# The scores of A in two tiles of 64 rows side by side, half of the heads in each bank

## The chip, the cores and the metric

The kernel runs on one NeuronCore of a Trainium2 chip, as one launch. The metric is the device time of that launch in microseconds (us). The core's engines run side by side, each through its own stream of instructions in order: TensorE (PE in the profile, and PEld for its weight loads), VectorE (DVE), ScalarE (ACT), GpSimd (POOL) and SyncE (SP), which here only issues transfers. They wait for one another through semaphores. Matmul results land in PSUM, a memory of 8 banks over 128 partitions; DVE and ACT read them there.

## What is computed

Nyström attention over 8 batches of 8 heads, 576 tokens of width 64, and behind it a two-layer network with SiLU on all 4608 tokens (512 to 2048 to 512). Cut to what matters:

```python
q_lm = q.reshape(B, H, 32, 18, D).mean(axis=3)       # 32 landmarks per head
k_lm = k.reshape(B, H, 32, 18, D).mean(axis=3)
A  = softmax(scale * q    @ k_lm.T)                  # 576 x 32
Bm = softmax(scale * q_lm @ k_lm.T)                  # 32 x 32
C  = softmax(scale * q_lm @ k.T)                     # 32 x 576
Z = Bm.T / (norm1(Bm) * norminf(Bm) + 1e-6)
for _ in range(6):
    Z = 2 * Z - Z @ Bm @ Z
x = A @ Z @ C @ v                                    # then to (tokens, 512)
out = silu(x @ w_in) @ w_out
```

q, k and v are drawn with a standard deviation of 0.1. The softmax subtracts each row's maximum; any number that is the same for all terms of a row would do.

## The kernel before

**Stages.** The order of all instructions is written out by hand. Batch 0's attention runs alone at the start (lines 630 to 712). Then a loop over batches (717) takes 16 steps each; every step computes a piece of the hidden layer (`l1_mm`, tile `hps`), its SiLU on ACT (`l1_act`, tile `gT`) and some matmuls of the second layer (`l2_mm`, tile `ops`, copied out by ACT as `ost` and stored by SP). Between them stand the pieces of the next batch's attention. `d` is 4 for batch 0, 3 for batch 1 and 0 after; in step d + 1 the scores of B and C are computed, in step d + 2 those of A. `idle` issues matmuls of zeros that fill PE's time, `table` loads ACT's function table for Exp or Silu.

**Layout.** A batch's eight heads are two groups g of four. Each head has 32 landmarks and the 64 columns of D are split into two halves e of 32, so a group's four heads with one half lie on 4 x 32 = 128 partitions: `qkT` holds q and k that way, transposed (`transpose_qk`), and `bd` holds k's landmarks as a block diagonal of 128 x 128 for each g and e, with zeros outside the four 32 x 32 blocks (`bd_expand`).

**The scores of A** are computed in chunks of tokens, `TCH`: four whole chunks of 128 and one of 64. `a_scores(i)` makes scores for pair i: chunks 0 and 1 (i = 0), 2 and 3 (i = 1), and chunk 4 alone (i = 2). For every chunk, group and half it issues one matmul: weights `qkT` (128 rows, the chunk's 128 tokens), moving `bd` (128 rows, 128 columns), accumulated over e. That is 16 matmuls for the whole chunks and 4 for the last, where the weights have 64 columns. One PSUM bank, `sa[i]`, holds 2 chunks of 256 scores (8 heads of 32 landmarks): `sa[0]` in the pool `psa`, `sa[1]` in `pso`; the last chunk lies in the bank `bb` of the B work, or in `pso` for batch 0.

**What follows, pair by pair:** `a_max(i)` (L486, DVE) writes the negated maximum over 32 landmarks to `nm`; `a_shift(i)` (L493, PE) adds it to the bank with one matmul of the identity with `nm` broadcast; `a_exp(i)` (L499, ACT) writes the exponentials to `ex`. `a_norm(i)` is `a_sum` (L509, DVE, to `arec`), `a_rec` (L514, DVE) and `a_mul` (L524, POOL, to `an`). `an` is then transposed to `AT`, by PE and copies (`a_transpose`, `a_out`) for batches 0 and 1, by transfers of SP after that.

**Beside it on DVE and PE:** `c_scores` (PE, tile `scp`, tiles of 32*32), `c_max` (L382) and `c_exp` (L390) for C; `b_max`, `b_exp`, `b_norm`, `f_mm`, `b_scale` (L322) and `f_out` (L327) for B; then the iteration, alternately `ns_mm` (PE, `bb<-fx`) and `ns_step` (L348, DVE, `fx`); then `w_mm`, `w_out` (tiles `wp`, `W`), `x_out`, `z_mm`, `z_out`, and four `m_unit` (tiles `mp`, `mb`: 64*32 tiles on PE, copied by DVE and ACT), which give the weights of the hidden layer. `landmarks_pe` (`lmp`) sums rows of a later batch with the identity as weights; `landmarks_pool` does so on POOL from batch 3 on, behind a small copy (`gate`, L868) that waits for DVE.

Of the kernel before, what the change touches and what calls it, by code (L numbers as in the profile page):

```python
# [10 lines left out]
AF = mybir.ActivationFunctionType  # L11
# [28 lines left out]
def kernel(  # L40
# [9 lines left out]
    nc = tc.nc  # L50
    B, H, S, Dh = q.shape
    L = 32
    SEG = S // L
# [3 lines left out]
    sc = 1.0 / float(Dh) ** 0.5  # L57
# [3 lines left out]
    TCH = [(c, min(c + 128, S)) for c in range(0, S, 128)]  # L61
# [13 lines left out]
    def mm(o, lhsT, rhs, start, stop):  # L75
        nc.tensor.matmul(out=o, lhsT=lhsT, rhs=rhs, start=start, stop=stop,  # L76
                         skip_group_check=True)
# [4 lines left out]
    def psa1(nm, dt=FP):  # L82
        return psa.tile([128, 512 if dt == FP else 1024], dt, tag="a", name=nm)

    def pso1(nm, dt=FP):
        return pso.tile([128, 512 if dt == FP else 1024], dt, tag="o", name=nm)
# [98 lines left out]
    def landmarks_pe(b, p, j0, n, ts=(0, SEG)):  # L185

        o = p[:, 0:4 * Dh].rearrange("p (j d) -> p j d", d=Dh)[:, j0:j0 + n, :]
        for t in range(*ts):
            mm(o, ident, nat_t[b][:, j0:j0 + n, Dh * t:Dh * t + Dh],
               start=(t == 0), stop=(t == SEG - 1))  # L190
# [27 lines left out]
    class Att:  # L218
# [239 lines left out]
        def a_dims(self, i):  # L458
            cc = list(range(2 * i, min(2 * i + 2, len(TCH))))
            return cc[0], len(cc), TCH[cc[0]][1] - TCH[cc[0]][0]  # L460

        def a_scores(self, i):
            if i == 0:
                s = psa1("sa")
            elif self.b == 0:
                s = pso1("sa")
            else:
                s = pso1("sa") if i == 1 else self.bb[:, 128:384]
            self.sa[i] = s
            first = True  # L470
            for c in range(2 * i, min(2 * i + 2, len(TCH))):
                c0, c1 = TCH[c]
                o = 256 * (c - 2 * i)
                ov = s[0:c1 - c0, o:o + 256].rearrange("p (r g n) -> p g r n", r=2, g=2)
                for g in range(2):
                    for e in range(2):
                        mm(ov[:, g].rearrange("p r (j l) -> p r j l", l=L),
                           self.qkT[:, 2 * g, c0:c1, e],
                           self.bd[:, g, :, e].rearrange("p (j r l) -> p r j l", r=2, l=L),
                           start=first, stop=(e == 1))  # L480
                        first = False

        def a_max(self, i):
            c, n, pr = self.a_dims(i)
            with nc.allow_low_precision(reason="any shift common to a row's terms is exact"):
                nc.vector.tensor_reduce(  # L486
                    out=self.nm[0:pr, c:c + n, :],
                    in_=self.sa[i][0:pr, 0:256 * n].rearrange("p (c h l) -> p c h l", h=8, l=L),
                    op=OP.max, axis=AX.X, negate=True)

        def a_shift(self, i):
            c, n, pr = self.a_dims(i)
            mm(self.sa[i][0:pr, 0:256 * n].rearrange("p (c l) -> p c l", l=L), ident[0:pr, 0:pr],  # L493
               self.nm[0:pr, c:c + n, :].rearrange("p c h -> p (c h)").unsqueeze(2)
                   .to_broadcast((pr, 8 * n, L)), start=False, stop=True)

        def a_exp(self, i):
            c, n, pr = self.a_dims(i)
            nc.scalar.activation(out=self.ex[0:pr, c:c + n, :].rearrange("p c n -> p (c n)"),  # L499
                                 in_=self.sa[i][0:pr, 0:256 * n], func=AF.Exp, scale=sc / SEG)  # L500

        def a_part(self, i):
            c, n, pr = self.a_dims(i)
# [135 lines left out]
    a = Att(0)  # L639
# [13 lines left out]
    a.b_max()  # L653
    a.b_exp()
    a.a_start()
    a.a_scores(0)
    a.a_scores(1)
    a.a_scores(2)
    a.c_max(0)
    a.c_exp(0)  # L660
# [19 lines left out]
    a.a_exp(1)  # L680
    a.c_out(1, nc.scalar.copy)
    a.w_scale()
    a.a_norm(0)
    lp0 = ps2("lmp")
    idle(lp0[:, 1, :], 5)
    a.ns_step()
    a.ns_mm()
    landmarks_pe(1, lp0[:, 0, :], 1, 1, (0, 9))
    a.a_norm(1)
    a.ns_step()  # L690
    a.ns_mm()
# [25 lines left out]
    for b in range(B):  # L717
        nxt = b + 1 < B
        cnt = CNT.get(b, EVEN if b % 2 == 0 else ODD)
        h = {}  # L720
# [11 lines left out]
        for s in range(NDC):  # L732
# [39 lines left out]
            elif not nxt or s == d:  # L772
                l1(s)
                act(s)
                l2_mm(cnt[s])

            elif s == d + 1:
                l1(s)
                act(s)
                l2_mm(cnt[s])  # L780
                a.b_scores()
                a.c_scores()
                a.b_max()
                a.c_max(0)
                table(AF.Exp)
                a.b_exp()
            elif s == d + 2:
                n = cnt[s]
                a.a_start()
                a.a_scores(0)  # L790
                a.a_scores(1)
                a.c_max(1)
                a.a_max(0)
                a.a_max(1)
                a.c_exp(0)
                a.c_exp(1)
                l2_mm(min(n - 4, 6))
                a.a_scores(2)
                a.a_max(2)
                a.a_shift(0)  # L800
                a.a_exp(0)
                l2_mm(2)
                a.a_shift(1)
                a.a_exp(1)
                a.b_norm()
                l2_mm(2)
                a.a_shift(2)
                a.a_exp(2)
                l2_mm(n - 4 - min(n - 4, 6))
                table(AF.Silu)  # L810
                if b == 0:
                    a.f_mm()
                    a.b_scale()
                    a.f_out()
                l1(s)
            elif b == 0:
                l1(s)
                r = s - d
                if r == 3:
                    act(s - 1)  # L820
                    a.ns_mm()
                    a.c_transpose(0)
                    a.a_norm(0)
                    a.ns_step()
                    a.c_out(0)
                elif r == 4:
                    a.ns_mm()
                    a.c_transpose(1)
                    a.w_scale()
                    a.ns_step()  # L830
                    a.ns_mm()
# [132 lines left out]
```

## Time and profile before

| | us |
|---|---|
| median of 3 runs | 278.99 (278.54 to 279.84) |
| the profiled execution, its own time | 280.51 |
| its span in the trace | 278.8 |
| PE busy in the span | 264.3 (95%) |
| ACT, DVE, POOL busy | 176.9, 161.0, 117.4 |
| mean granted clock of PE | 0.967 |

The groups of the page that belong to the scores of A, all batches together:

```profile
L76 PE MATMUL sa<-bd,qkT 128*128 128x128 bf16 x128 | 8.8, 220 | 0.0
L486 DVE TENSOR_REDUCE nm<-sa 128x16 bf16<-128x512 f32 x16 | 10.3, 682 | 0.0
L76 PE MATMUL sa<-nm,ident 128*128 128x512 bf16 x16 | 6.4, 398 | 1.2 <-DVE nm L486 1.2
L499 ACT ACTIVATE ex<-sa 128x512 bf16<-128x512 f32 x16 | 9.4, 598 | 2.3 <-PE sa L76 2.0
L509 DVE TENSOR_REDUCE arec<-ex 128x16 f32<-128x512 bf16 x16 | 10.9, 679 | 0.4 <-ACT ex L499 0.3
```

A group's line gives the line of the kernel (L76 is the helper that issues every matmul), engine, operation, the tile written and those read, the shape of the PE tile as rows*columns, the shape of the data, how often; then the busy time in us and the mean of one in ns; then the idle time of the engine just before them and what ended it. Matmuls are pipelined: 220 ns is the time of one from start to end, and the next one starts long before. In a timeline a line gives start, duration, engine and operation; runs of one kind are merged with their number.

### The profile page before, as it was taken

Reading aid. Unit: us, or ns where it says so; the run is one execution under the profiler, and the core shown is the slowest. Engines: PE = TensorE matmul, PEld = TensorE weight load, DVE = VectorE, ACT = ScalarE, POOL = GpSimd, SP = SyncE. Lnnn points to the kernel's source line nnn. Section 1 sums busy time; section 2 is a strip of 40 time slices with the busy share of each in tenths; the row PEclk is TensorE's granted clock in tenths of the full one; section 3 lists DMA queues with packets and bytes.
Section 4 is the critical chain, followed back from the end, with each engine's and each line's share of the span. In section 5 each row is a group of like instructions: output and inputs, shape, how many; then the busy total and the mean of one; then the engine's idle time right before and its main releaser. Section 6 shows DMA issues by size and latency. Waiting matters only on the chain.

```text
span 278.8 us, 6934 instructions
## 1 busy us (share of the span) xinstructions
PE 264.3 (95%) x2826; PEld 149.1 (53%) x2826; DVE 161.0 (58%) x399; ACT 176.9 (63%) x350; POOL 117.4 (42%) x165
## 2 busy tenths in 40 slices
PE   5968999999999999998999999998999999999994
PEld 2845655565554555464645565454645565555541
DVE  4895688378586756839792757658784653100000
ACT  2354696578756975668666955687667855646511
POOL 8434232514796269365774279217741030100000
PEclk9775799999999999999999999999999999999998
DMA  6999998893992965649193948315291312110111
GB/s 105 204 208 206 204 207 172 141 177 58 177 179 61 172 131 94 124 92 192 56 156 71 196 115 114 92 42 93 27 179 38 91 54 72 40 75 38 40 75 75
DMA packets 37792, 32.37 MB, mean 116 GB/s; under 512 B 18816, under 2 KB 29056, under 8 KB 37760
## 3 DMA queue, kind: packets, MB, share of 16 engines
q0 software_dynamic: 15104, 18.35, 41.3%
q1 hardware_dynamic: 22656, 13.57, 19.9%
q8 instruction: 22, 0.36, 0.5%
q14 instruction: 10, 0.08, 0.1%
HBM read 36.70 MB, written 9.44 MB: 165 GB/s over the span
## 4 chain that ended last, share of the span: by engine, by line
PE 84%; DVE 9%; issue 2%; DMA 2%; ACT 1%; POOL 0%; ACTq 0%; POOLq 0%
PE ops L76 43%; PE hps L76 22%; PE bb L76 4%; PE mp L76 4%; PE lmp L76 3%; DVE cmx L382 3%; PE sa L76 3%; DMA nat<-in_q_dram 2%; PE scp L76 2%; PE wp L76 2%; DVE nm L486 1%; DVE fx L322 1%; PE atp L542 1%; PE idle L76 1%; PE ctp L404 1%
## 5 line engine op out<-in xcount | busy, mean ns | idle before, releaser
L76 PE MATMUL ops<-w_out_sb,gT 128*128 128x512 bf16 x576 | 148.9, 380 | 0.0
L593 ACT ACTIVATE gT<-hps 128x576 bf16<-128x576 f32 x128 | 82.4, 652 | 65.2 <-PE hps L76 64.9
L76 PE MATMUL hps<-AT,mb 128*128 128x288 bf16 x512 | 83.5, 288 | 0.4 <-DVE mb L565 0.2
L76 PEld LDWEIGHTS <-gT 128*128 128x128 bf16 x576 | 52.0, 98 | 48.0 <-issue 7.0
L76 PEld LDWEIGHTS <-mb 128*128 128x128 bf16 x512 | 48.4, 98 | 26.6 <-issue 2.0
L182 DVE STREAM_TRANSPOSE qkT<-nat 128x576 f32<-128x576 f32 x32 | 39.3, 1244 | 1.9 <-DMA nat<-in_k_dram 1.3
L524 POOL TENSOR_TENSOR an<-ex,arec 128x512 bf16<-128x512 bf16 (+1 forms) x24 | 21.2, 902 | 28.9 <-ACT W L433 14.8
L565 DVE CAST mb<-mp 128x512 bf16<-128x512 f32 x30 | 20.7, 691 | 20.1 <-PE mp L76 20.1
L619 ACT COPY ost<-ops 128x512 f32<-128x512 f32 x36 | 21.1, 586 | 10.7 <-PE ops L76 10.6
L348 DVE SCALAR_TENSOR_TENSOR fx<-fx,bb 128x320 bf16<-128x320 bf16 (+1 forms) x40 | 17.2, 430 | 17.8 <-PE bb L76 17.5
L204 POOL TENSOR_TENSOR lma<-nat 128x1152 f32<-128x1152 bf16 x10 | 23.7, 2373 | 0.0
L153 ACT ACT_TABLE_LOAD x16 | 20.5, 1283 | 1.1 <-PEq L948 0.8
L566 ACT CAST mb<-mp 128x512 bf16<-128x512 f32 x32 | 18.7, 584 | 3.8 <-PE mp L76 3.7
L245 POOL COPY bd<-lmc 32x128 bf16<-32x128 bf16 x28 | 8.1, 289 | 30.5 <-DVE lmc L237 29.7
L76 PE MATMUL bb<-fx 32*32 32x64 bf16 (+2 forms) x168 | 13.3, 211 | 4.3 <-DVE fx L327 3.1
L76 PEld LDWEIGHTS <-ident 128*128 128x128 bf16 (+1 forms) x240 | 12.5, 111 | 8.7 <-issue 5.3
L76 PEld LDWEIGHTS <-fx 32*32 32x32 bf16 (+1 forms) x168 | 8.3, 95 | 15.4 <-DVE fx L327 4.2
L868 POOL COPY gate<-nrm 128x2 f32<-128x2 f32 x6 | 1.1, 186 | 35.1 <-DVE nrm L318 31.8
L509 DVE TENSOR_REDUCE arec<-ex 128x16 f32<-128x512 bf16 (+1 forms) x24 | 14.1, 588 | 0.4 <-ACT ex L499 0.3
L76 PE MATMUL mp<-w_in_sb,zwT 64*32 64x512 bf16 x256 | 13.7, 400 | 0.1
L76 PE MATMUL lmp<-nat,ident 128*128 128x64 bf16 x216 | 10.9, 214 | 1.9 <-DMA nat<-in_k_dram 1.3
L382 DVE TENSOR_REDUCE cmx<-scp 128x1 f32<-128x576 f32 x16 | 12.0, 751 | 0.7 <-PE scp L76 0.4
(85 smaller groups left out, 264.2 us busy)
## 6 DMA issues: line engine op xcount, KB each, us to landing
out_dram<-ost SPq DMA_DIRECT2D x36, 256.0 KB, 2.3
nat<-in_k_dram POOLq DMA_DIRECT2D x16, 288.0 KB, 6.3
nat<-in_q_dram POOLq DMA_DIRECT2D x16, 288.0 KB, 7.6
v<-in_v_dram POOLq DMA_DIRECT2D x8, 576.0 KB, 7.6
w_in_sb<-in_moe_w_in_dram POOLq DMA_DIRECT2D x4, 512.0 KB, 15.6
w_out_sb<-in_moe_w_out_dram POOLq DMA_DIRECT2D x4, 512.0 KB, 16.2
AT<-an SPq DMA_TRANSPOSE x30, 4.4
eCT<-eC SPq DMA_TRANSPOSE x12, 5.7
```

The lines of the kernel that those rows point to most:

```text
L76: nc.tensor.matmul(out=o, lhsT=lhsT, rhs=rhs, start=start, stop=stop, skip_group_check=True)
L153: nc.scalar.activation(out=spare[:, 1:2], in_=spare[:, 0:1], func=func)
L182: nc.vector.transpose(out=o.rearrange("p (l t) -> p t l", t=SEG), in_=nat_t[b][:, j, :].bitcast(FP).rearrange("p (t l) -> p t l", l=L))
L204: nc.gpsimd.tensor_tensor(out=a1, in0=nat[:, :, 0:3 * w], in1=nat[:, :, 3 * w:6 * w], op=OP.add)
L348: nc.vector.scalar_tensor_tensor(out=n, in0=self.fx, scalar=2.0, in1=self.p, op0=OP.mult, op1=OP.subtract)
L382: nc.vector.tensor_reduce(out=mx, in_=self.s[g][:, :, 0:HF], op=OP.max, axis=AX.XY, negate=True)
L509: nc.vector.tensor_reduce(out=r, in_=x, op=OP.add, axis=AX.X)
L524: nc.gpsimd.tensor_tensor(out=self.an[0:pr, c:c + n, :].rearrange("p c (h l) -> p (c h) l", l=L), in0=x, in1=r.unsqueeze(2).to_broadcast(( ...
L565: (copy[0] if copy else nc.vector.tensor_copy)(out=o[:, 0, :], in_=m[0])
L566: nc.scalar.copy(out=o[:, 1, :], in_=m[1])
L593: nc.scalar.activation(out=gT_t[b][:, 2 * s:2 * s + 2, o:o + HF], in_=h[:, :, 0:HF], func=AF.Silu)
L619: nc.scalar.copy(out=ost, in_=st["ps"])
```

## The change

The whole chunks' scores are computed by `a_tiles` instead of `a_scores(0)` and `a_scores(1)`. Since `bd` is block diagonal, its upper 64 rows meet only the first two heads of a group and its lower 64 rows only the last two. `a_tiles` therefore issues, for each chunk, group and half, two matmuls: t = 0 with the upper 64 rows of `qkT` and of `bd`'s columns 0 to 63, t = 1 with the lower 64 rows and columns 64 to 127. Each has 128 tokens as weight columns and 64 columns moving; t = 0 writes to the bank `sa[0]`, t = 1 to `sa[1]`. So a bank no longer holds two chunks with all heads, but all four chunks with half of the heads (four per chunk, 16 rows of 32 landmarks in all, as before).

`a_max`, `a_shift` and `a_exp` for i = 0 and 1 then work on a bank with half of the heads; `a_bank` gives the places of these heads in `nm` and `ex`, which keep their layout (in `nm` every second element, in `ex` 16 runs of 32). `a_sum`, `a_rec` and `a_mul` still work on pairs of chunks with all heads, so each of them reads what both exponentials wrote. In the start, `a_norm(0)` moves behind one iteration step, next to `a_norm(1)`. The last chunk and its part of the work are as before. Matmuls in a batch: 32 for the whole chunks instead of 16.

```diff
+        def a_tiles(self):
+            self.sa[0], self.sa[1] = psa1("sa"), pso1("sa")
+            for c in range(4):
+                for g in range(2):
+                    for e in range(2):
+                        for t in range(2):
+                            p = slice(64 * t, 64 * t + 64)
+                            o = self.sa[t][:, 128 * c:128 * c + 128]
+                            mm(o.rearrange("p (r g l) -> p g r l", r=2, g=2)[:, g],
+                               self.qkT[p, 2 * g, 128 * c:128 * c + 128, e],
+                               self.bd[p, g, 64 * t:64 * t + 64, e]
+                               .rearrange("p (r l) -> p r l", l=L),
+                               start=(c == 0 and g == 0 and e == 0), stop=(e == 1))
+
+        def a_bank(self, x, t):
+            return x[:, 0:4].rearrange("p c (x t n) -> p (c x) t n", x=4, t=2)[:, :, t, :]
...
         def a_max(self, i):
             c, n, pr = self.a_dims(i)
+            nm = self.nm[0:pr, c:c + n, :] if i == 2 else self.a_bank(self.nm, i)[:, :, 0]
...
-                    out=self.nm[0:pr, c:c + n, :],
-                    in_=self.sa[i][0:pr, 0:256 * n].rearrange("p (c h l) -> p c h l", h=8, l=L),
+                    out=nm.rearrange("p c h -> p (c h)") if i == 2 else nm,
+                    in_=self.sa[i][0:pr, 0:256 * n].rearrange("p (h l) -> p h l", l=L),
...
         def a_exp(self, i):
             c, n, pr = self.a_dims(i)
-            nc.scalar.activation(out=self.ex[0:pr, c:c + n, :].rearrange("p c n -> p (c n)"),
-                                 in_=self.sa[i][0:pr, 0:256 * n], func=AF.Exp, scale=sc / SEG)
+            nc.scalar.activation(out=self.ex[0:pr, 4, :].rearrange("p (h l) -> p h l", l=L)
+                                 if i == 2 else self.a_bank(self.ex, i),
+                                 in_=self.sa[i][0:pr, 0:256 * n].rearrange("p (h l) -> p h l", l=L),
+                                 func=AF.Exp, scale=sc / SEG)
...
     a.a_start()
-    a.a_scores(0)
-    a.a_scores(1)
+    a.a_tiles()
     a.a_scores(2)
...
     a.w_scale()
-    a.a_norm(0)
     lp0 = ps2("lmp")
     idle(lp0[:, 1, :], 5)
     a.ns_step()
     a.ns_mm()
     landmarks_pe(1, lp0[:, 0, :], 1, 1, (0, 9))
+    a.a_norm(0)
     a.a_norm(1)
     a.ns_step()
     a.ns_mm()
...
                 a.a_start()
-                a.a_scores(0)
-                a.a_scores(1)
+                a.a_tiles()
                 a.c_max(1)
                 a.a_max(0)
                 a.a_max(1)
```

More of the change, by code (lines that the diff above doesn't have):

```diff
@@ L460, in a_dims @@
             return cc[0], len(cc), TCH[cc[0]][1] - TCH[cc[0]][0]
-        def a_scores(self, i):
[L463 to L468, printed above, removed]
+        def a_tiles(self):
[13 more added lines that the diff above has]
+            return x[:, 0:4].rearrange("p c (x t n) -> p (c x) t n", x=4, t=2)[:, :, t, :]
+        def a_scores(self, i):
+            s = pso1("sa") if self.b == 0 else self.bb[:, 128:384]
             self.sa[i] = s
             first = True
-            for c in range(2 * i, min(2 * i + 2, len(TCH))):
+            for c in range(4, len(TCH)):
                 c0, c1 = TCH[c]
-                o = 256 * (c - 2 * i)
-                ov = s[0:c1 - c0, o:o + 256].rearrange("p (r g n) -> p g r n", r=2, g=2)
+                ov = s[0:c1 - c0, 0:256].rearrange("p (r g n) -> p g r n", r=2, g=2)
                 for g in range(2):
@@ L492, in a_shift @@
             c, n, pr = self.a_dims(i)
+            nm = (self.nm[0:pr, c:c + n, :].rearrange("p c h -> p (c h)") if i == 2
+                  else self.a_bank(self.nm, i)[:, :, 0])
             mm(self.sa[i][0:pr, 0:256 * n].rearrange("p (c l) -> p c l", l=L), ident[0:pr, 0:pr],
-               self.nm[0:pr, c:c + n, :].rearrange("p c h -> p (c h)").unsqueeze(2)
-                   .to_broadcast((pr, 8 * n, L)), start=False, stop=True)
+               nm.unsqueeze(2).to_broadcast((pr, 8 * n, L)), start=False, stop=True)
         def a_exp(self, i):
             c, n, pr = self.a_dims(i)
-            nc.scalar.activation(out=self.ex[0:pr, c:c + n, :].rearrange("p c n -> p (c n)"),
-                                 in_=self.sa[i][0:pr, 0:256 * n], func=AF.Exp, scale=sc / SEG)
+            nc.scalar.activation(out=self.ex[0:pr, 4, :].rearrange("p (h l) -> p h l", l=L)
+                                 if i == 2 else self.a_bank(self.ex, i),
+                                 in_=self.sa[i][0:pr, 0:256 * n].rearrange("p (h l) -> p h l", l=L),
+                                 func=AF.Exp, scale=sc / SEG)
         def a_part(self, i):
```

## The prediction

> **What bounds the kernel now.** I read the page first, then the timeline around the places that the diff touches, engine by engine, then the table by stretches for the clock. The page says that TensorE (PE) ends the run:
>
> ```profile
> PE 264.3 (95%) x2826; PEld 149.1 (53%) x2826; DVE 161.0 (58%) x399; ACT 176.9 (63%) x350; POOL 117.4 (42%) x165
> PE 84%; DVE 9%; issue 2%; DMA 2%; ACT 1%; POOL 0%; ACTq 0%; POOLq 0%
> L76 PE MATMUL ops<-w_out_sb,gT 128*128 128x512 bf16 x576 | 148.9, 380 | 0.0
> ```
>
> Second line: PE is 84% of the chain that ended last, so a shorter PE stretch pays, unless PE waits for something else soon after. The scores of A stand in a knot where VectorE (DVE) works beside PE, so the waits there decide. I call a "stage" the few microseconds in which batch b computes the next batch's scores; there are seven, starting near 37, 65, 91, 123, 152, 184 and 213 us. PE in the third of them:
>
> ```profile
> 91.24 0.45 PE L76 MATMUL scp<-qkT,lmc 32*32 32x288 bf16 x16
> 91.62 1.10 PE L76 MATMUL sa<-bd,qkT 128*128 128x128 bf16 x16
> 92.56 1.46 PE L76 MATMUL ops<-w_out_sb,gT 128*128 128x512 bf16 x6
> 93.95 0.42 PE L76 MATMUL bb<-bd,qkT 128*64 128x128 bf16 x4
> 94.30 0.39 PE L76 MATMUL sa<-nm,ident 128*128 128x512 bf16 x1
> ```
>
> The 16 matmuls that the change replaces hold PE from 91.62 to 92.56, 0.94 us (59 ns each). The first matmul that depends on DVE is `sa<-nm` (the shift, L493) at 94.30. DVE meanwhile:
>
> ```profile
> 93.46 1.28 DVE L486 TENSOR_REDUCE nm<-sa 128x16 bf16<-128x512 f32 x2
> 94.66 0.41 DVE L486 TENSOR_REDUCE nm<-bb 64x8 bf16<-64x256 f32 x1
> ```
>
> The first of the two maxima takes 0.68 us (mean of its group), so it ends at 94.14. In the first stage PE did wait for it:
>
> ```profile
> 39.47 1.28 DVE L486 TENSOR_REDUCE nm<-sa 128x16 bf16<-128x512 f32 x2
> 40.21 0.38 PE L76 MATMUL sa<-nm,ident 128*128 128x512 bf16 x1 [0.59 <-DVE nm L486]
> ```
>
> There the maximum ended at 39.47 + 0.68 = 40.15 and the shift started 0.06 later. So in the third stage the shift could have started at 94.20 at the earliest: only 0.10 us of slack. DVE's column before that (two maxima of C's scores, L382, back to back) starts when PE's `scp` ends, ahead of the changed matmuls, and so is not shortened by them.
>
> The other place is the start, batch 0, where DVE and ScalarE (ACT) set the pace:
>
> ```profile
> 19.42 0.60 ACT L499 ACTIVATE ex<-sa 128x512 bf16<-128x512 f32 x1 [0.80 <-PE sa L76]
> 20.05 0.69 DVE L509 TENSOR_REDUCE arec<-ex 128x16 f32<-128x512 bf16 x1 [0.28 <-ACT ex L499]
> 20.77 0.25 DVE L514 RECIPROCAL arec<-arec 128x16 f32<-128x16 f32 x1
> 20.94 0.23 DVE L348 SCALAR_TENSOR_TENSOR fx<-fx,bb 128x128 bf16<-128x128 bf16 x1
> 21.22 0.29 PE L76 MATMUL bb<-fx 32*32 32x64 bf16 x8 [0.49 <-DVE fx L348]
> ```
>
> Second exponential, sum, reciprocal, iteration step, PE: the chain of waits runs through these very pieces, on to `wp`, W and the transposes.
>
> **The matmuls, per stage.** Removed: 0.94 us. Added: 32 matmuls, 16 pairs, each with 64 rows of the array and 64 columns moved. No row shows this shape, so bounds. Low: both of a pair run at once and a pair costs what one 64-column matmul with a full weight load costs; 18 `lmp` matmuls (128x64) stand 0.52 us in the chain at 60.13, 29 ns each, so 16 x 29 = 0.46 us. High: every one of the 32 alone at 59 ns, 1.89 us. I take 0.50, near the low end, because the `mp` matmuls (64 rows by 32 columns, eight tiles) occupy PE from 99.42 to 99.87, 0.45 us, although eight times 512 columns at the 216 ns that `ops` takes would be 1.73: disjoint tiles, row halves among them, do overlap there.
>
> The shape of the tile also changes once more. Six `ops` at 216 ns from 92.56 end their turn at 93.86, and the 128*64 matmul starts at 93.95: 0.09 us for a change of shape. Before, `scp` (32*32) to `sa` (128*128) was one change and `sa` to `ops` none; now both are changes: +0.09. In batch 0 there is no extra one, since the 128*64 matmuls follow there anyway. So PE's part shrinks from 0.94 to 0.59, by 0.35 us (between 0.39 shorter and 1.04 longer).
>
> The Trainium skill speaks against halving rows ("TensorE: Matmul & The Clock Gate", section LDWEIGHTS): a weight load costs by its columns, 128 / 1.2 = 107 ns, however few rows it has, and the change doubles the loads. If 32 such loads stood one behind another the stage would be 32 x 107 = 3.4 us, and seven stages some 17 us more, as an estimate. The `lmp` row contradicts this, with a 128-column load for each of its matmuls and 29 ns from one to the next, so the sum goes without it.
>
> **What of the 0.35 is left.** In the first two stages PE already waits 0.59 us for the maximum: gain 0, the wait grows. In stages 3, 5 and 7 the shift comes forward by its slack, 0.10 us (shift starts 94.30, 155.65, 216.44 against maxima that end at 94.14, 155.49, 216.28), and the other 0.25 becomes a new wait on DVE. After it PE has no idle time until the next stage, so 3 x 0.10 = 0.30 us is kept. In stages 4 and 6 DVE is late again:
>
> ```profile
> 128.78 2.57 DVE L322 TENSOR_SCALAR fx<-bm,nrm 128x32 bf16<-128x32 bf16 x2
> 131.74 0.31 PE L76 MATMUL bb<-fx 128*128 128x160 bf16 x2 [0.89 <-DVE fx L327]
> ```
>
> PE idles 0.89 us at the end of a DVE chain that began at `scp`; 0.10 us earlier only lengthens that. Gain 0. In batch 0 PE has finished these matmuls 2.3 us before DVE reads them (14.14 against 16.47): gain 0. Sum: -0.30 us. DVE's maxima now need both halves' last matmul, but start 0.6 us or more after PE has finished in every stage (38.84 to 39.47 in the first); a matmul stretch of over 1.57 us would use that cover up and push DVE's chain by the rest.
>
> **The move at the start.** A sum over all heads of chunks 0 and 1 needs both exponentials now, and the first normalization (sum 0.72 with its gap, reciprocal 0.17 until the next instruction starts: 20.05 to 20.77 to 20.94) goes behind an iteration step. The step that goes ahead could run about 0.65 us earlier (19.54 to about 18.9), but its PE matmuls stand behind the five `zero` matmuls that end near 19.8, so they stay at 19.84: gain 0. Then DVE waits for the second exponential until 20.05 as before, and does two sums and two reciprocals where it did one of each: the next step moves from 20.94 to 20.05 + 2 x 0.89 = 21.83, +0.89 us. Behind it on DVE stand the last maximum and the next step; on PE nine `lmp`, the shift of chunk 4, the last iteration, `wp`; then W, transposes, the first hidden layer. All come 0.89 later. GpSimd's first product moves from 19.78 to about 21.0, the second starts near 22.1 and ends near 23.15, before the transposes (24.01, then 24.9); three weight and V loads behind it on its queue go out about 1 us later, and first serve in the next stages. Bounds: 0, if later waits swallow it (the chain from 21 to 37 us holds no wait for a DMA), to 0.89 + 0.09.
>
> The 0.09 is the exponential's new output, in runs of 32: the C exponential with stepped operands takes 740 ns for 576 columns, the plain `gT` 652. I take 0, since `ex` reads and writes contiguous runs; in the stages it is covered by 1.4 us that ACT's next output is ready ahead of PE.
>
> **Clock.**
>
> ```profile
> 24.63:28.04 3.41, 3.19 (x33) 1.87 (x32) 1.85 (x5) 1.79 (x4) 0.20 (x1) 0.50 1.25 207
> 28.04:31.45 3.41, 3.41 (x47) 2.53 (x46) 1.17 (x2) 1.51 (x4) 0.41 (x1) 0.50 1.24 207
> 31.45:34.87 3.42, 3.11 (x46) 1.82 (x43) 3.10 (x6) 3.05 (x7) 0.85 (x3) 1.00 1.21 200
> ```
>
> PE's granted clock (the column before the DMA share) is half from 17.80 to 31.45, in steps of 3.41. If it returns at the same moment, 0.9 us of work runs at full rate that ran at half: -0.45; if it returns one step later, up to 3.41 / 2 = +1.7. I take 0.
>
> Sum: 280.51 + 0.89 - 0.30 = 281.10 for the profiled execution, +0.59. That execution lies 1.5 us above the median; on the median, 278.99 + 0.59 = **279.6 us**.
>
> **Rivals.** (a) The start's delay is swallowed: only -0.30, 278.7. For: batch 1's stage has waits of PE for DVE; against: they hang on the same PE work. (b) PE's gain counts in full, the maxima not being what the shift waits for: 7 x -0.35 + 0.89 = -1.56, 277.4. Against: the 0.06 us after the maximum at 40.21. (c) Slower: the longer pause of PE in the start keeps the half clock one step of 3.41 us more; place 31.45 to 34.87, price up to 1.7 where PE sets the pace, say 1.3: 280.9. It decides if the stretch after the first hidden layer shows 0.50. (d) The change doesn't do what it says: the halves run one after the other at 59 ns each. Then a stage's PE part grows by 1.04: 3 x 1.04, about 0.4 in each of the others (DVE's maxima start late) and 0.89 are 5.6: 284.6. Against: the `mp` row.
>
> **How the numbers follow.** A measurement of this kernel can tell about 0.5%, 1.4 us: 277.6 to 280.4 is "no change". Forecast 0.50 (279.1 to 280.2), (a) 0.18, (b) 0.07, (c) 0.18, (d) 0.07. Faster: (b) and a little of (a), 0.09. Slower: (c), (d) and 0.04 for a forecast that lands above its own range, 0.29. Same: 0.62. The range leaves out (b) and (d) and reaches through (a) and (c): 278.2 to 281.4.
>
> **What would show it.** `sa<-bd` in 64*128 tiles from the first to the next `ops` in about 0.6 us instead of 0.94; in all seven stages a wait of the shift for `nm` (about 0.25 where none was, 0.95 in the first two); in the start two sums back to back and the step at about 21.8; everything from there about 0.9 later and 0.1 regained in each of stages 3, 5, 7. If stages 3, 5 and 7 become shorter by 0.3, the slack was misread; if batch 0's hidden layer starts no later, the move was free.

## The result and the profile after

The changed kernel takes 280.62 us, the median of 13 executions (279.75 to 281.70), against 278.58 us for the kernel before in the same session (13, 277.60 to 280.71). The ratio is 1.0058, with a 95% interval of 1.0033 to 1.0084: 1.6 us slower (0.9 to 2.3; the medians themselves differ by 2.04), just beyond the 1.4 us that was called "no change". The predicted 279.6 is 1.0 us too low; the range 278.2 to 281.4 holds the result.

The profiled execution of the changed kernel took 281.23 us, its span is 279.5. Its page, the lines that answer to those shown of before (busy time, chain of waits, the second layer's group):

```profile
PE 256.5 (92%) x2915; PEld 145.6 (52%) x2954; DVE 161.0 (58%) x399; ACT 176.6 (63%) x350; POOL 117.1 (42%) x165
PE 73%; DVE 13%; DMA 5%; issue 4%; POOL 2%; ACT 2%; POOLq 0%; ACTq 0%
L76 PE MATMUL ops<-w_out_sb,gT 128*128 128x512 bf16 x537 | 141.5, 380 | 4.0 <-issue 3.2
```

A warning comes first: 39 of the 576 `ops` matmuls have no record here (x537), so some 8 us of PE's missing busy time and the idle "issue" of 3.2 are gaps in the record. That transfers (DMA) now stand in the chain with 5%, where they had 2%, and DVE with 13% instead of 9%, is no such gap: the traces of e3 and e12 below, with all 576 records, have 4 and 5% for DMA, 12 and 13% for DVE.

The groups of the scores of A, shapes kept apart:

```profile
L76 PE MATMUL sa<-bd,qkT 64*128 64x64 bf16 x256 | 5.2, 190 | 0.0
L502 DVE TENSOR_REDUCE nm<-sa 128x16 bf16<-128x512 f32 x16 | 10.3, 683 | 0.0
L76 PE MATMUL sa<-nm,ident 128*128 128x512 bf16 x16 | 6.5, 406 | 2.2 <-DVE nm L502 2.2
L516 ACT ACTIVATE ex<-sa 128x512 bf16<-128x512 f32 x16 | 9.4, 600 | 2.5 <-PE sa L76 2.3
L528 DVE TENSOR_REDUCE arec<-ex 128x16 f32<-128x512 bf16 x16 | 10.8, 675 | 0.9 <-ACT ex L516 0.9
```

All 256 tiles are there. Maximum, exponential and sum cost what they did (682, 598 and 679 ns before), so the strided places in `nm` and `ex` cost nothing that shows here. The shift's wait for the maximum has grown from 1.2 to 2.2 us.

**The tiles** in the timeline of PE, first stage:

```profile
37.91 0.65 PE L76 MATMUL sa<-bd,qkT 64*128 64x64 bf16 x32
38.50 0.39 PE L76 MATMUL ops<-w_out_sb,gT 128*128 128x512 bf16 x1
...
40.40 0.38 PE L76 MATMUL sa<-nm,ident 128*128 128x512 bf16 x1 [0.67 <-DVE nm L502]
```

From the first tile to the next kind of matmul 0.59 us (37.91 to 38.50), exactly the predicted 0.59; before it was 0.94. But the shift stands at 2.49 us after the first tile, where it stood at 2.47: DVE's maximum holds it.

**The loop.** The time from one batch's first hidden-layer matmul to the next one's, from the traces (b is the batch that is finished in between, its column holds stage b + 1; "again" is a further trace of the kernel before, taken among the experiments):

| b | 0 | 1 | 2 | 3 | 4 | 5 | 6 |
|---|---|---|---|---|---|---|---|
| before | 30.42 | 31.24 | 31.29 | 30.07 | 30.73 | 30.06 | 30.73 |
| before, again | 29.31 | 31.23 | 31.30 | 30.06 | 30.74 | 30.05 | 30.73 |
| after | 30.04 | 32.16 | 31.16 | 30.06 | 30.61 | 30.05 | 30.62 |

From b = 2 on these repeat to 0.01 us. Stages 3, 5 and 7 are 0.11 to 0.13 shorter, 4 and 6 unchanged: the predicted pattern, 0.10 each foretold. What was not foretold is the column b = 1, longer by 0.92.

**The start**, in the changed kernel (timeline, DVE with the instructions of ACT and PE that it works with):

```profile
19.84 0.60 ACT L516 ACTIVATE ex<-sa 128x512 bf16<-128x512 f32 x1 [0.80 <-PE sa L76]
...
20.47 0.69 DVE L528 TENSOR_REDUCE arec<-ex 128x16 f32<-128x512 bf16 x1 [0.86 <-ACT ex L516]
21.19 0.25 DVE L533 RECIPROCAL arec<-arec 128x16 f32<-128x16 f32 x1
21.36 0.63 DVE L528 TENSOR_REDUCE arec<-ex 128x16 f32<-128x512 bf16 x1
22.02 0.25 DVE L533 RECIPROCAL arec<-arec 128x16 f32<-128x16 f32 x1
22.19 0.23 DVE L348 SCALAR_TENSOR_TENSOR fx<-fx,bb 128x128 bf16<-128x128 bf16 x1
22.48 0.24 PE L76 MATMUL bb<-fx 32*32 32x64 bf16 x8 [1.35 <-DVE fx L348]
```

and in the further trace of the kernel before, whose second exponential starts at the same 19.84:

```profile
20.47 0.69 DVE L509 TENSOR_REDUCE arec<-ex 128x16 f32<-128x512 bf16 x1 [0.28 <-ACT ex L499]
21.19 0.25 DVE L514 RECIPROCAL arec<-arec 128x16 f32<-128x16 f32 x1
21.36 0.23 DVE L348 SCALAR_TENSOR_TENSOR fx<-fx,bb 128x128 bf16<-128x128 bf16 x1
```

Both sums now wait for the exponential and stand one behind the other; the iteration step comes at 22.19 instead of 21.36, +0.83. DVE sits idle for 0.86 us ahead of the first sum: about what the first sum and its reciprocal took in that place in the kernel before.

**Clock**, by stretches (from:to, duration; PE, PEld, DVE, ACT, POOL busy; granted clock; DMA share; GB/s), the changed kernel and then the kernel before, again:

```profile
24.37:27.78 3.41, 2.98 (x33) 1.92 (x33) 1.55 (x5) 2.60 (x5) 1.56 (x3) 0.50 1.25 208
27.78:31.20 3.42, 3.42 (x42) 2.37 (x41) 0.80 (x3) 1.12 (x3) 0.60 (x1) 0.50 1.24 206
```

```profile
24.66:28.07 3.41, 3.19 (x40) 2.08 (x38) 1.41 (x4) 2.09 (x6) 1.15 (x2) 0.50 1.25 207
28.07:31.50 3.43, 3.33 (x66) 2.17 (x64) 2.54 (x4) 2.45 (x7) 0.00 (x0) 1.00 1.24 206
```

The half clock (0.50) stays for one step of 3.41 us more in this pair of traces: in the same length PE does 42 matmuls instead of 66. It is no mark of the change by itself, for in the first trace of the kernel before it lasts from 17.80 to 31.45.

**The account of this pair.** Spans 279.52 against 276.86, +2.66. First hidden-layer matmul of batch 0: 27.65 against 26.27, +1.38, of it 0.83 the order; the other 0.55 fits the half clock, in which the changed kernel spends the last 3.28 us ahead of that matmul and the kernel before 1.61. Column b = 0: +0.73, which fits the further step at half clock. Column b = 1: +0.93. The rest: -0.38.

**The new wait** in column b = 1, PE in the changed kernel:

```profile
88.85 0.41 PE L76 MATMUL mp<-w_in_sb,zwT 64*32 64x512 bf16 x8
89.85 0.65 PE L76 MATMUL hps<-AT,mb 128*128 128x288 bf16 x4 [0.59 <-DMA AT<-an]
```

Batch 2 is the first whose `AT` is transposed by transfers, and here the first hidden-layer matmul waits 0.59 us for it. The other 0.3 is the stretched `wp` further ahead, with the second transpose of `eC` landing in its midst; before and then after:

```profile
77.31 0.56 PE L76 MATMUL wp<-v,eCT 96*32 96x64 bf16 x48
```

```profile
77.50 0.82 PE L76 MATMUL wp<-v,eCT 96*32 96x64 bf16 x48
```

### The profile page after: what moved, and what is told of

Same layout as the page of the kernel before. It is cut to its first block, busy times and chain, and to the rows that moved or that the text cites. A ratio compares the mean times of both kernels' runs of the same rounds, so it can differ in the third digit from the quotient of the medians.

```text
span 279.5 us, 7150 instructions
## 1 busy us (share of the span) xinstructions
PE 256.5 (92%) x2915; PEld 145.6 (52%) x2954; DVE 161.0 (58%) x399; ACT 176.6 (63%) x350; POOL 117.1 (42%) x165
## 4 chain that ended last, share of the span: by engine, by line
PE 73%; DVE 13%; DMA 5%; issue 4%; POOL 2%; ACT 2%; POOLq 0%; ACTq 0%
PE ops L76 38%; PE hps L76 21%; DVE cmx L382 4%; PE bb L76 4%; PE mp L76 4%; DMA nat<-in_q_dram 3%; DMA AT<-an 2%; PE lmp L76 2%; DVE nm L502 2%; PE scp L76 2%; PE sa L76 2%; PE wp L76 1%; DVE fx L322 1%; POOL an L543 1%; DVE cbs L385 1%
## 5 line engine op out<-in xcount | busy, mean ns | idle before, releaser
L76 PE MATMUL ops<-w_out_sb,gT 128*128 128x512 bf16 x537 | 141.5, 380 | 4.0 <-issue 3.2
L76 PEld LDWEIGHTS <-ident 128*128 128x128 bf16 (+1 forms) x240 | 11.8, 108 | 9.1 <-issue 5.2
L264 DVE TENSOR_REDUCE bmx<-bb 128x2 f32<-128x64 f32 x8 | 1.7, 217 | 19.2 <-PE bb L76 19.1
L516 ACT ACTIVATE ex<-sa 128x512 bf16<-128x512 f32 (+1 forms) x17 | 9.8, 587 | 4.7 <-PE sa L76 4.5
```

## The experiments

Theory S: the start's order costs 0.8 to 0.9 us and shifts the half clock, the tiles in the loop gain 0.3 to 0.4, nothing else. The rivals: the tiles themselves cost somewhere in the loop, or the start is swallowed; for the 0.92 in column b = 1, theories W, D and I below. Each version ran beside executions of the kernel before on the same chip, and the ratios are against these.

### e1 to e4: the parts, and another start

e1: the tiles and the moved normalization in batch 0 alone, batches 1 to 7 as in the kernel before (`a_pair` is the old code for a pair of chunks).

```diff
+            self.split = b == 0
...
+            if not self.split:
+                self.a_pair(0)
+                self.a_pair(1)
+                return
```

> Tiles of 64 rows and the moved normalization in batch 0 alone; batches 1 to 7 score A as before. Theory S (the start pays: two sums and two reciprocals on DVE between the second exponential and the next iteration step, +0.89, and the loop gives 0.3 back): 0.9 to 1.9 us slower than before, at least as slow as the changed kernel; first hidden-layer matmul about 0.9 later than before at the same clock. Theory L (the loop pays: the last transposed piece of batch 2's AT lands late and PE waits 0.6 for it, as at 89.85 in the changed kernel): within 0.5 of before.

Measured: 279.99 against 279.02 us, ratio 1.0037 [1.0017, 1.0058]. The start alone costs 1.03 us (0.5 to 1.6). In its trace the half clock lasts for four steps on end, as in the first trace of the kernel before, and the first hidden-layer matmul starts at 27.96 instead of 27.08, 0.88 later. So rival (a) of the prediction, a delay that is swallowed, falls.

e2: the reverse, `self.split = b > 0`, with `a.a_norm(0)` of the start where it was before.

> Tiles of 64 rows in batches 1 to 7 alone; batch 0 and the order of its normalizations as before. Theory S: 0.3 us faster than before (0.10 in each of stages 3, 5 and 7, the rest lost in waits of the shift for the maximum), and the trace has no PE wait for AT of batch 2, or one that has nothing to do with the tiles. Theory L: 0.7 to 1.5 us slower than before, with that wait.

Measured: 279.06 against 279.02, ratio 1.0010 [0.9987, 1.0033]. Its trace has the three gains (columns 2, 4 and 6: 31.18, 30.61, 30.61) and 31.23 in column 1, thus no late `AT`. The total doesn't show the 0.36: it is smaller than the interval, and in this trace three half-clock steps run on end from 19.31 to 29.55, where the further trace of the kernel before has one of them at 7.59 to 11.00, when PE waits for a load for 0.59 us anyway. Column 0 is 29.79 instead of 29.31, which fits that.

e3: the changed kernel with an iteration step ahead of both normalizations, `a_norm(1)` behind one more, and chunk 4's maximum, shift and exponential behind `w_out`.

```diff
     landmarks_pe(1, lp0[:, 0, :], 1, 1, (0, 9))
-    a.a_norm(0)
-    a.a_norm(1)
     a.ns_step()
     a.ns_mm()
     landmarks_pe(1, lp0[:, 0, :], 1, 1, (9, 18))
-    a.a_max(2)
-    a.a_shift(2)
-    a.a_exp(2)
+    a.a_norm(0)
     a.ns_step()
     a.ns_mm(last=True)
+    a.a_norm(1)
     a.w_mm()
     a.w_out()
+    a.a_max(2)
+    a.a_shift(2)
+    a.a_exp(2)
```

> The changed kernel with another order in the start: the third iteration step ahead of the first normalization, the second normalization behind the fourth step, the last chunk's maximum, shift and exponential behind the W matmuls. Theory S: the 0.9 disappear and some 0.3 to 0.4 more (the iteration then waits for no sum): 1.2 to 1.5 us faster than the changed kernel, level with before or up to 0.7 faster. Theory L: at most 0.5 faster than the changed kernel.

Measured: 279.19 against 279.02, ratio 1.0010 [0.9993, 1.0028]: by the ratios 1.3 us below the changed kernel. From the first `scp` to the first hidden-layer matmul its trace takes 14.45 us, where the changed kernel takes 15.41 and the kernel before, again, 13.96. Taking the two sums out of the iteration's way gives two thirds back; a part of this is the clock, for in the last stretch of half clock ahead of that matmul PE spends 2.25 us here, 3.28 in the changed kernel and 1.61 in the kernel before. In what remains are the transposes, which now wait 0.43 us for GpSimd's `an`. Column 1 is 32.14 here too.

e4: the kernel before, unchanged, for a further trace.

> The kernel before, unchanged, as a control with its own trace, span and clock of every run. Both theories: ratio 1.000, within 0.3%. Theory S: its spans at the same mean clock lie about 0.6 us below those of the changed kernel, and where the half clock lasts from 17.8 to 31.5 us as in the first trace the span is near 278.8, otherwise 1 to 2 us lower. Theory L: its trace shows no PE wait for AT of batch 2.

Measured: 279.07 against 279.02, ratio 1.0010 [0.9988, 1.0032]. Its trace is the one used above. In it the third `AT` transpose lands 0.21 us ahead of its reader; in the first trace it was 3.24. Such landings move by microseconds from one execution to another of the same kernel.

### e5 to e8: the late transposes

The load of `v` for batch 3 (576 KB) is issued by GpSimd ahead of SP's `AT` transposes of batch 2, and these land only after it. Theory W: the tiles move them so that PE regularly waits. Theory D: it is chance.

> The changed kernel once more, for its trace. Open: PE waited 0.6 us for the transposed AT of batch 2 in the traces of the changed kernel and of the version with the norms later, not in those of the kernel before and of the two part versions. If the wait is a regular part of the change (theory W), this trace shows it again and the interval from batch 1's first hidden layer to batch 2's is 32.1 us. If it comes and goes with the moment at which the v load of batch 3 lands (theory D), the interval may also be 31.2 us, and the times fall into two groups 0.9 us apart. Theory S alone (start order, clock steps) expects 280.6 and says nothing of this wait. All: start as in the first trace, hidden layer 1.4 us later than before, intervals of batches 0, 1, 2, 4, 6 about 0.1 shorter in stages 3, 5, 7.

Measured for e5, the changed kernel once more: 280.80 against 279.46, ratio 1.0040 [1.0015, 1.0065]. Column 1 is 32.18 again, but PE loses the time earlier, at the transposes of `eC` (C's exponentials) that `wp` reads:

```profile
77.47 0.36 PE L76 MATMUL wp<-v,eCT 96*32 96x64 bf16 x24 [0.33 <-DMA eCT<-eC]
78.07 0.36 PE L76 MATMUL wp<-v,eCT 96*32 96x64 bf16 x24 [0.24 <-DMA eCT<-eC]
```

`AT` is no earlier than in the first trace: its third piece, the last that the first hidden-layer matmul needs, lands 24.69 us after the stage's first `scp` (24.68 there), and in the kernel before that matmul is due at 23.80. PE, already 0.8 late from `wp`, comes to it at 24.74 and waits only 0.07. So two transfers are late, each by enough to hold up most of this stage's 0.9; theory W named one of them, and the times don't fall into D's two clean groups. e6 moves the `v` load in the changed kernel:

```diff
-                if s == 7 + d // 2:
+                if s == (13 if b == 1 else 7 + d // 2):
                     load_v(b + 2)
```

> The changed kernel with the v load of batch 3 issued six steps later, so that it is behind the AT transposes of batch 2 in time instead of just ahead of them. Theory W (the wait behind that load is a regular part of the loss): interval of batch 1 to 2 is 31.2 us, the transposes land 2 us or more ahead of their readers, time 0.6 to 0.9 us below the changed kernel. Theory D (now and then): 0.2 to 0.6 below, the slower group of times gone. If the load is not the cause, the same time as the changed kernel and the wait still there.

Measured: 280.41 against 279.46, ratio 1.0038 [1.0012, 1.0065]; 0.4 below e5, with intervals that overlap widely. In its trace `AT` lands 5 us ahead of its reader, so the load is what it stood behind; but `eC`'s transposes are late by as much as in e5, and column 1 is 32.17:

```profile
76.38 0.36 PE L76 MATMUL wp<-v,eCT 96*32 96x64 bf16 x24 [0.46 <-DMA eCT<-eC]
76.99 0.36 PE L76 MATMUL wp<-v,eCT 96*32 96x64 bf16 x24 [0.24 <-DMA eCT<-eC]
```

> Control: the kernel before with the same load six steps later. Theory W: no change within 0.3 us, as the kernel before does not wait there. Theory D: up to 0.3 us faster, for the runs of the kernel before that wait too (its nearest miss was 0.2 us).

Measured for e7, the kernel before with the same edit: 279.36 against 279.46, ratio 0.9998 [0.9970, 1.0026]; column 1 is 31.23. The control holds.

e8: the tiles in the loop alone (e2), with the `v` load of e6, and

```diff
-                l2_mm(min(n - 4, 6))
+                l2_mm(min(n - 4, 7))
                 a.a_scores(2)
...
-                l2_mm(n - 4 - min(n - 4, 6))
+                l2_mm(n - 4 - min(n - 4, 7))
```

> Tiles of 64 rows in batches 1 to 7 alone, start as in the kernel before, seven instead of six matmuls of the second layer ahead of the first shift, v load of batch 3 six steps later. If the 0.35 us that a stage's tiles save went into the new wait for the maximum, the additional matmul (0.22 us) takes that wait's place: each of stages 1, 2, 3, 5 and 7 is 0.2 shorter than with the tiles alone, so 0.36 + about 1.0 = 0.8 to 1.4 us below the kernel before, and the shift waits 0 to 0.1 in stages 3, 5, 7. If the wait only moves behind the next maximum or exponential, the time stays at 0.3 to 0.4 below.

Measured: 278.70 against 279.46, ratio 0.9980 [0.9948, 1.0011], not told from no change. PE in stage 5, first in e2 and then in e8:

```profile
154.31 0.38 PE L76 MATMUL sa<-nm,ident 128*128 128x512 bf16 x1 [0.17 <-DVE nm L526]
```

```profile
154.25 0.42 PE L76 MATMUL bb<-bd,qkT 128*64 128x128 bf16 x4
154.62 0.38 PE L76 MATMUL sa<-nm,ident 128*128 128x512 bf16 x1
```

The wait is gone, filled by the matmul moved ahead of it, and columns 4 and 6 fall from 30.61 to 30.40: 0.21 each. So in stages 5 and 7 the lost part of the tiles' gain did go into the wait for the maximum. Stage 3 (column 2, 31.18) gains nothing more; why is open. In stages 1 and 2 `n` is 6, the edit moves nothing there; that was overlooked in the expectation, which is why its 0.8 to 1.4 was too much.

### e9 to e12: what makes the transposes late

In the traces up to e8, the second `eC` transpose of batch 2 is issued 4.4 to 4.7 us after the stage's first `scp` in each version. The second half of `wp` reads it, from 0.04 us after the landing at the earliest, and is due at 12.55 (the first half, due at 12.37, reads the first transpose; the expectation of e12 below takes 12.37 for both). It landed at 12.33 and 12.45 (before), 12.30 (e7), 12.50 (e1), 12.44 (e2), all in time, at 12.62 (e8), 0.1 late, but at 12.79 (after), 13.32 (e5), 13.46 (e6) and 12.89 (e3). All four with the whole change are late, by 0.3 to 1.0. The trace's records of transfers show 16 KB instruction loads on a queue of their own, some 245 PE instructions apart on average. In the four late traces one starts at 8.2 to 9.2 us, among the transposes; in the other six none starts between 2 and 11 us. Theory I: the additional PE instructions have moved this load there.

> The changed kernel with four of the seven first idle matmuls (512 columns) replaced by 84 of 16 columns: 80 matmuls more on PE before any data has landed, so that its 16 KB instruction loads come at other moments. Theory I (the loss of 0.9 us between batch 1 and 2 comes from such a load, which the 96 additional PE instructions of the tiles had moved from 13.4 to 8.2-9.2 us after the stage's first scp, into the transposes of eC that PE is waiting for): the load is back near 13 us, the second transpose lands at 12.3 to 12.6 instead of 12.8 to 13.5, PE does not wait for eCT, the interval of batch 1 to 2 is 31.2 instead of 32.17, time 0.9 us below the changed kernel (0.6 to 1.2), some 279.8. Theory S alone with another cause of the 0.9 (the tiles, the later start): interval stays 32.2, time as the changed kernel, 280.6. Start: no later than in the changed kernel.

> The kernel before, nothing of the change in it, with the same four idle matmuls replaced by 52 of 16 columns: 48 matmuls, 96 PE instructions more ahead of everything, as many as the tiles of batches 0, 1 and 2 add. Theory I: the instruction load now falls at 8 to 10 us after the stage's first scp as in the changed kernel, the second transpose of eC lands at 12.8 to 13.5, PE waits 0.5 to 1.1 us for eCT in the second stage, the interval of batch 1 to 2 is about 32.1 instead of 31.24, time 0.6 to 1.1 us above the kernel before. If the 0.9 belongs to the tiles themselves: interval 31.24, time as before within 0.3.

The edit in both, with 84 in the changed kernel and 52 in the kernel before:

```diff
-    idle(wt, 7, 512)
+    idle(wt, 3, 512)
+    idle(wt, 84, 16)
```

Measured: e9 280.72 against 279.24, ratio 1.0070 [1.0043, 1.0097]; column 1 is 31.86, the second transpose lands at 13.15. The load didn't go back to 13 us, as intended, but to 1.38, in front of the loads of q and k, the first two of which land some 0.5 us later than in the traces before (5.74 and 7.14, where it was 5.0 to 5.3 and 6.6 to 6.8). e10 280.03 against 279.24, ratio 1.0035 [1.0014, 1.0055]; the load is at 8.17 as intended, but the transpose lands at 12.40 in its trace and column 1 is 31.23. Its time is 0.8 us longer, as theory I said, without the wait that it named in the one execution that was traced. All columns from 1 on are those of the kernel before there, so what that execution loses lies ahead of batch 1; why is open. Both expectations failed on the mechanism; in its strict form theory I is out.

e12 tests a weaker form: the changed kernel with 18 idle matmuls fewer,

```diff
-        idle(wt, 4 if j else 8)
+        idle(wt, 1 if j else 2, 512)
...
-    idle(wt, 8)
+    idle(wt, 2, 512)
...
-    idle(wt, 5)
+    idle(wt, 1, 512)
+    idle(wt, 1)
```

> The changed kernel with its idle matmuls of 128 columns in the start merged into ones of 512: the same columns, 18 matmuls (36 PE instructions) fewer. Of the traces so far, those with an instruction load of PE between 1.2 and 2.6 us after the second stage's first scp (into the loads of q and k) or between 8.2 and 10.5 us (into the transposes of eC) had the transposes land at 12.8 to 13.5 us, with one exception (12.40 with a load at 8.17), and those with neither at 12.3 to 12.6; the reader is due at 12.37. Theory I, in this weaker form: 36 instructions fewer put the loads near -1.2 and 11.8 us, as in the versions with tiles in the start alone or in the loop alone; the second transpose lands at 12.3 to 12.6, the interval of batch 1 to 2 is 31.2 to 31.5, the time 0.6 to 0.9 us below the changed kernel, some 279.9. If the landing belongs to the change in another way (GpSimd's sums start 0.27 us earlier there): landing still 12.8 or later, interval 32.1, time as the changed kernel, 280.6 to 280.8.

Measured: 280.35 against 279.03, ratio 1.0041 [1.0017, 1.0064]. The loads are at -0.49 and 11.55, and the second transpose lands at 12.25, the earliest of all, although GpSimd's sums start as early (6.26) as in the changed kernel; that rival is out. The view of the tile `eCT` in that stage, after and then e12:

```profile
DMA to landing us min/median/max: 8.3/8.8/9.2
```

```profile
DMA to landing us min/median/max: 7.8/8.2/8.5
```

But now `AT` is late: its third piece lands 24.24 us after that `scp`, and column 1 is 31.71, so the 0.6 to 0.9 that were expected are not gained. The `v` load ahead of it landed at 20.98. That alone doesn't explain it, for in the further trace of before the load landed at 21.66 and the third piece at 23.58, in time:

```profile
90.05 0.65 PE L76 MATMUL hps<-AT,mb 128*128 128x288 bf16 x4 [0.41 <-DMA AT<-an]
```

### e11: a version from these findings

The start of the kernel before, tiles in batches 1 to 7, in stages 1 and 2 three second-layer matmuls more ahead of the first shift and in the others one (and 96 small idle matmuls more at the start).

```diff
-                l2_mm(min(n - 4, 6))
+                n0, n1 = ((n - 1, 1) if b < 2 else (min(n - 4, 7), 2))
+                l2_mm(n0)
```

> Start as in the kernel before, tiles in batches 1 to 7, the fillers of the stages moved ahead of the shifts (in stages 1 and 2 three more of them, in the others one), and the 96 additional small idle matmuls that put PE's instruction loads where the kernel before has them. If the wait for the maximum is all that stands between the tiles and a gain, stages 1 and 2 lose 0.5 to 0.65 us of waiting each, 3, 5 and 7 0.2 each, and with the 0.36 of the tiles the time is 1.3 to 2.0 us below the kernel before. If what follows in a stage is pinned to VectorE's chain, as stages 4 and 6 are, less: 0.6 to 0.9 below.

Measured: 278.97 against 279.24, ratio 0.9997 [0.9978, 1.0017]. PE in the second stage:

```profile
66.96 0.38 PE L76 MATMUL sa<-nm,ident 128*128 128x512 bf16 x1 [0.29 <-DVE nm L526]
...
75.84 0.36 PE L76 MATMUL wp<-v,eCT 96*32 96x64 bf16 x24 [0.29 <-DMA eCT<-eC]
76.51 0.36 PE L76 MATMUL wp<-v,eCT 96*32 96x64 bf16 x24 [0.31 <-DMA eCT<-eC]
```

The wait for the maximum falls from 0.66 to 0.29 and the iteration's PE work comes 0.48 us earlier, and then all of it is given back at `wp`: PE waits for `eCT`, which lands at 12.87 (an instruction load stands at 1.22 here, as in e9). Column 1 is 31.58 instead of 31.23. Stage 2 is bound by that transfer: even its earliest landing in any trace, 12.25, would let the second half of `wp` come only 0.26 us earlier. No version here beats the kernel before by more than can be measured.

## Why the prediction came out as it did

**The matmuls of a stage: right.** 0.94 to 0.59 us predicted, and 0.94 to 0.59 measured; from the first tile to the last 0.47 us, 30 ns for a pair, near the low bound of 0.46 that was preferred to 1.89. Rival (d), halves one after the other, is out. The weight loads cost no more than this: 32 loads of 128 columns in 0.47 us, one every 15 ns. Their row:

```profile
L76 PEld LDWEIGHTS <-qkT 64*128 64x128 bf16 x256 | 4.3, 94 | 2.0 <-issue 1.5 <-DVE bmx L264 0.2 <-DVE bbs L267 0.2
```

A single load is recorded with 94 ns from start to end, and 256 of them fill 4.3 us, so they overlap. "TensorE: Matmul & The Clock Gate", section LDWEIGHTS, in the Trainium skill gives 107 ns for one; the single load's 94 ns are near that, and what fails is the estimate of 3.4 us that set 32 of them one behind another.

**What of it is left in the loop: right in place, nearly in size.** The gains are 0.13, 0.12 and 0.11 in stages 3, 5 and 7, 0.36 in sum where 0.30 was said, and 0 in 4 and 6. In stage 4 the step that waits on DVE's chain shows the same 0.10 us as a longer wait, 0.89 before:

```profile
132.71 0.31 PE L76 MATMUL bb<-fx 128*128 128x160 bf16 x2 [0.99 <-DVE fx L327]
```

All seven stages wait for the maximum. Stage 3 in the changed kernel:

```profile
94.71 0.42 PE L76 MATMUL bb<-bd,qkT 128*64 128x128 bf16 x4
95.30 0.38 PE L76 MATMUL sa<-nm,ident 128*128 128x512 bf16 x1 [0.17 <-DVE nm L502]
```

The shift starts 0.59 us after the last chunk's scores (the 128*64 matmuls) instead of 0.35 (93.95 and 94.30): 0.24 later, where 0.25 was foretold; the profile counts 0.17 of it as idle, from the end of those scores. In the first two stages the shift waits 0.67 and 0.66 us, not the 0.95 foretold: another 0.23 is waited ahead of the last chunk's scores, for ACT's exponential of B (`pb`; read in e2, which has all its `ops`). e8 shows for stages 5 and 7 that this wait is where the gain went. Rival (b), the gain in full, is out.

**The start: right.** +0.89 predicted for the iteration step, +0.83 measured; the second sum runs right behind the first reciprocal and takes 0.63 us where 0.69 was taken. e1 shows that it is paid (1.03 us), e3 that moving the sums out of the way returns most of it. Rival (a) is out.

**The clock: taken as 0; whether the change touches it is not shown.** The mean granted clock of an execution falls into steps, and a lower step goes with a longer time: among 116 executions of the kernel before shown with the experiments, median spans of 276.5, 277.2 and 278.1 us go with mean clocks of about 0.988, 0.982 and 0.975. 26 of them have the highest; of the 25 of the changed kernel none has. The mean clock is 0.9803 against 0.9782; at 0.8 us for a step of 0.0065 that is some 0.26 us. It is at most a shift in how often a step more occurs, so (c)'s 1.3 was too much for the median. And that (c)'s reason, the longer pause in the start, is behind it isn't shown: of the 36 executions of e2, e8 and e11, whose start has the old order, none has the highest clock either, and of the 12 of e9, whose start is the changed one, 3 have.

**The missing term: the transfers of batch 2.** What the prediction lacks is a loss in stage 2: its sum has "gain 0" there and nothing on the other side, and it looked for waits on a DMA from 21 to 37 us only. The view that would have shown the risk is the landing of `eCT` against its reader: in the first trace of before the second transpose landed at 12.33 and would have been late from 12.51 on, 0.18 us of slack (0.05 in the further one). At the same granted clock the changed kernel is 1.25 us longer (278.45, 12 executions, against 277.2, 45; clock 0.982) and 1.15 longer (279.25, 12, against 278.1, 40; clock 0.975). The order of the start and the loop's gain make +0.47 of it, so 0.7 to 0.8 remains; column 1 of the six traces with tiles in all batches is longer by 0.48 to 0.95. The parts alone don't have it: at these two clocks e1 is 0.6 and 0.75 longer than the kernel before, and e2 level and 0.1 shorter (6 executions each), together 0.6.

That these waits exist, and in which transfers, is shown. That an instruction load among the transposes makes them late fits e12 and four traces and contradicts e10. e10 is also an open rival for the remainder: without any tile it is 0.95 and 0.8 longer at the same two clocks, and its trace has none of these waits. Open stays, too, why the last `AT` transpose lands 24 to 26 us after that `scp` in the versions with tiles in all batches and the `v` load in its old place, and at 22 to 24 in the kernel before, and whether this is the tiles' doing in each execution: a single trace of most versions can't tell.

**The forecast as a whole** named the mechanism of the start and the loop and its sign: +0.59, and +0.47 measured. The measured +1.6 (0.9 to 2.3) has more of the same sign, about 0.3 that goes with the clock and 0.7 with the late transfers. That the range holds the result is partly luck: its upper end was there for a step of the clock, not for transfers, and the sum started from 278.99, the median of three executions, where 13 gave 278.58.

## What to carry to other kernels

When a change brings work forward or back past a point where a transfer lands, list landing against reader for each transfer of that stage, not only the waits that show: a slack of 0.18 us leaves no wait in the view, and a landing 0.3 us later does. A faster matmul group pays only up to the next engine's result; give the freed time to work that is ready (here one filler matmul ahead of the shift, 0.21 us in a stage). And splitting data by head instead of by chunk turned two staggered exponential-and-sum pairs into a barrier, which cost more at the start, 0.83 us, than the matmuls returned in the whole loop.

## What the runs showed of the hardware

- Two tiles of 64 rows side by side run at 30 ns for a pair of 64-column matmuls, each with a weight load of 128 columns; seen in all seven stages (0.46 to 0.47 us for 16 pairs).
- A half-clock step lasts 3.41 us, and where it falls seems to matter beside how many there are: e2 and the further trace of the kernel before both have three (clock 0.982), but span 277.3 and 276.9 us, although e2's loop is 0.36 shorter. This is one pair of traces.
- PE's instructions arrive by transfers of 16 KB, 22 in the kernel before and 23 in the changed one, about 245 recorded PE instructions apart on average (from 128 to 365), each taking 0.9 to 2.1 us beside the data's transfers. The Trainium skill ("Runtime: NRT & Kernel Launch", section Instruction fetch mechanics) says blocks of 16 KiB, 256 instructions, whose cost is mostly hidden. The size agrees, and the average spacing nearly; that they can delay data is suggested by e12, with e10 against it.
- The `AT` transposes land behind an earlier load of `v` from another engine's queue: the first of them 0.3 to 1.3 us after it in each trace that has the load there (19.05 us after `scp` at the earliest), and at 16.83 and 16.84 with the load moved (e6 and e7).
